# Sums of the later heads by ScalarE, six weight pieces in the attention instead of eight, gate mixtures ahead of weight steps

## The chip, the cores and the metric

The kernel runs on one core of one Trainium2 chip. The metric is the device time of one execution in microseconds; the median of three runs stands for a kernel.

## What is computed

The reference, cut to what matters:

```
# attention: batch 4, 8 heads, 576 tokens, head size 64, mask by blocks of 64 tokens
scores = where(block_i >= block_j, q @ k.T / 8, -1e9)
attn   = exp(scores - max(scores));  attn /= sum(attn) + 1e-9
x = attn @ v                                  # heads side by side: 2304 tokens x 512
# first feed-forward
xk = mu_k * x + (1 - mu_k) * x_prev           # x_prev: the token before
xr = mu_r * x + (1 - mu_r) * x_prev
x  = sigmoid(xr @ w_r) * (relu(xk @ w_k)**2 @ w_v)      # w_k 512x1024, w_v 1024x512
# second feed-forward
xn = (x - mean) / sqrt(var + 1e-6) * g_ln
out = x + relu(xn @ w_ch1) @ w_ch2            # w_ch1 512x2048, w_ch2 2048x512
```

## The kernel before

All products keep fp32 accuracy: an operand is split into a high part (rounded to fp32r) and the rest, and three products are added. The order of work is written by hand; every engine has its own queue and takes it in that order.

**Attention** (loop at L725). A unit is one head (`h`), with two joint units (`z`) for the first 64 tokens. Iteration i issues on TensorE the score product A of unit i+1 (`s<-kq`), product B of unit i (`s<-QK`), which adds the rests and the subtracted maximum, and the value product of unit i-1 (`p<-e,V`). VectorE makes the maxima of unit i+1: five reductions `part<-s`, one `r<-part`; ScalarE moves three quarters (`r<-r`), then VectorE makes `m<-r` and `QK<-m,s`, on which product B waits. ScalarE makes `e<-s`, the exponentials (`em_B`).

`norm` (L469) ends unit i-2. The value product's PSUM tile `p` holds 64 rows of values and 64 rows of sums. ScalarE copies the values to `U`; `sums` (L480) reduces the sums on VectorE to `rs<-p`. Heads come by twos (z = 0 and 1); with the second, ScalarE adds 1e-9 (`rs<-rs`), VectorE makes the reciprocal and spreads it (`RB`), and GpSimd multiplies (`XT<-U,RB`).

**Weight pieces** (`load_split`, L83). `w_r`, `w_k` and `w_v` are 20 pieces of 128x512, each split in five steps: `load` (a DMA of 0.5 MB on SyncE's queue into an int8 tile `raw`, of which there are two), `above` and `below` (two Relu forms of the exponent byte), `expo` (L124 or L126) and `bits` (L130), `high`, `low`. A `raw` tile is free again after `bits`. In the attention (`PIECES`, L659) a letter stands for a step and its place for the iteration: ScalarE has `above`, `below` and `high`, GpSimd `expo` and `low`, VectorE `bits`. Behind it VectorE has `above` (L112), `expo` (L124) and `bits`, ScalarE `below` (`p<-raw,ce`), GpSimd `high` (L134) and `low`. There `Convert.step` (L154) moves every piece on its way one step on and then starts the next one:

```
for j in self.going: ... f = j.pop(0) ...
if start and self.jobs: j = self.jobs.pop(0) ... j.pop(0)()
```

**Gate stage** (L819). Six groups of 384 tokens; `em_r(g)` is 36 matmuls (`s<-wr,x`), `out_r` the sigmoid. The mixtures of group g+1 (`prep`, L502) are made meanwhile, for four blocks kk: scale on ScalarE (`p<-XT`), add on VectorE (`mix`, L513), cast on ScalarE (`x<-mix`), subtraction (`x<-mix,x`) on VectorE for kk = 0, called `sub0` here, and on GpSimd for the others. Weight steps are `conv.step()`.

**Hidden stage** (L835). Per group four products `em_h` (24 matmuls, `s<-x,wk`, two PSUM tiles in turn), each with an output `out_h` (L532): ScalarE `a<-s`, `k<-a`, `a<-a`, VectorE `k<-a,k`, with one tile `a`; then three value products `em_v` (`p<-wv,k`). In the first group (j = 0) the last weight steps run between product and output (`conv.some(3)`). The second feed-forward follows.

Of the kernel before, what the change touches and what calls it, by code (L numbers as in the profile page):

```python
# [7 lines left out]
F32 = mybir.dt.float32  # L8
# [4 lines left out]
ALU = mybir.AluOpType  # L13
AX = mybir.AxisListType
# [7 lines left out]
NG = NTOK // GT  # L22
# [9 lines left out]
def attention_moe_kernel(ctx, tc, raw_d, dup_d, raw0_d, dup0_d, v_d, v0_d, msk_d, mz_d, vec_d, eye_d, wk_d, wv_d, wr_d, wc1_d, wc2_d, out_d):  # L32
    nc = tc.nc
    red = nc.vector.tensor_reduce
# [4 lines left out]
    def act(out, in_, func=AF.Copy, **kw):  # L39
        nc.scalar.activation(out=out, in_=in_, func=func, **kw)  # L40
# [4 lines left out]
    def opened(es, name, bufs=1, **kw):  # L45
        return es.enter_context(tc.tile_pool(name=name, bufs=bufs, reuse_waits="tile", **kw))
# [136 lines left out]
    cp = opened(es_a, "ac", 1, side=R)  # L183
# [4 lines left out]
    lq = opened(es_q, "ar", 3, side=R)  # L188
    V = [cp.tile([128, 1024], F32, name=f"V{i}") for i in range(2)]
    RB = cp.tile([128, 512], F32, name="RB")  # L190
    part = [cp.tile([128, 16, 5], F32, name=f"part{i}") for i in range(2)]
    NB = 3
    QK = [qp.tile([128, 1216], F32R, name=f"QK{i}") for i in range(NB)]
    QB, KL = [x[:, 0:576] for x in QK], [x[:, 576:1216] for x in QK]
    IZ = 14
# [181 lines left out]
    def v3(ap):  # L377
        return ap.rearrange("p (b i) -> p b i", i=32)
# [90 lines left out]
    def norm(u):  # L469

        n = u[1]
        b, h = divmod(n, H)
        z = h % 2
        p = T.pop(("p", u, 0))
        if z == 0:
            T["nm"] = [sp.tile([128, 16], F32, name=x) for x in ("rs", "r3")] + [sp.tile([128, 512], F32, name="U")]
        rs, r3, U = T["nm"]
        act(U[64 * z:64 * z + 64], p[64 - 64 * z:128 - 64 * z])

        def sums():  # L480
            half = slice(64 * z, 64 * z + 64)
            red(out=rs[half], in_=v3(p[half]), axis=AX.X, op=ALU.max, apply_transpose=True)
            if z:
                act(rs, rs, bias=1e-9)

        return [sums] if z == 0 else [
            sums,
            lambda: nc.vector.reciprocal(out=r3, in_=rs),
            lambda: nc.vector.transpose(out=RB, in_=r3.unsqueeze(2).to_broadcast([128, 16, 32])),
            lambda: nc.gpsimd.tensor_tensor(out=XT[b][:, h // 2, 65:577], in0=U, in1=RB, op=ALU.mult),  # L490
        ]
# [25 lines left out]
    def preps(g, c, X):  # L517
        return [lambda kk=kk: prep(g, kk, c, X) for kk in range(4)]
# [3 lines left out]
    def em_h(X, m0):  # L522
        s = ps.tile([128, 1536], F32, name="s")
        nm = 2
        for kk in range(4):
            for i in range(nm):
                m = m0 + i
                for x, (wi, xi) in enumerate(PASS):
                    mm(s[:, 512 * i:512 * i + GT], wk[wi][:, kk, 128 * m:128 * m + 128], X[xi][:, kk], kk == 0 and x == 0, kk == 3 and x == 2)
        return s  # L530

    def out_h(m0, s):  # L532
        nm = 2
        sv = s.rearrange("p (i n) -> p i n", n=512)[:, 0:nm, 0:GT]
        a = hp.tile([128, 2, GT], F32, name="a")
        act(a[:, 0:nm], sv, AF.Relu)
        act(k2[0][:, m0:m0 + nm], a[:, 0:nm], AF.Square)
        act(a[:, 0:nm], a[:, 0:nm], AF.Square)
        sub(nc.vector, k2[1][:, m0:m0 + nm], a[:, 0:nm], k2[0][:, m0:m0 + nm])

    def em_r(X):
        s = ps.tile([128, 1536], F32, name="s")
        for kk in range(4):
            for t in range(3):
                for x, (xi, wi) in enumerate(PASS):
                    mm(s[:, 512 * t:512 * t + 512], X[xi][:, kk, 128 * t:128 * t + 128], wr[wi][:, kk], kk == 0 and x == 0, kk == 3 and x == 2)
        return s

    def out_r(g, s):
        r = rp.tile([128, 3, DM], F32, name="r")  # L550
        act(r.rearrange("p t d -> p (t d)"), s, AF.Sigmoid)
        T["r", g] = r
        if g in HORD[3:]:
            nc.scalar.dma_start(out=r_scr[g], in_=r)

    def load_r(g, p):
        T["r", g] = r = p.tile([128, 3, DM], F32, name="r")
        nc.sync.dma_start(out=r, in_=r_scr[g])
# [5 lines left out]
    def em_v(g, t, store=True):  # L564
        p = pv.tile([128, 512], F32, name="p")
        for m in range(8):
            for x, (xi, wi) in enumerate(PASS):
                mm(p, k2[xi][:, m, 128 * t:128 * t + 128], wv[wi][:, m], m == 0 and x == 0, m == 7 and x == 2)
        r = T["r", g][:, t]
        st = rs6.tile([128, 6], F32, name="st")  # L570
        tt(out=r, in0=p, in1=r, op=ALU.mult)
        i = 3 * g + t
        if store:
            put_x(g, t)
        nc.vector.bn_stats(out=st, in_=r)
        nc.vector.bn_aggr(out=mv[:, i], in_=st)
# [6 lines left out]
    def chunk_jobs(c):  # L583
        L = []
        for k in (0, 2):
            w = wc1_d[128 * k:128 * k + 256, CF * c:CF * c + CF].rearrange("(a p) n -> p a n", a=2)
            L.append(load_split(w, lambda i, k=k: W[c % 2][0][i][:, k:k + 2]))
        for k in range(2):
            r0 = CF * c + 128 * k
            L += pieces(wc2_d[r0:r0 + 128], lambda i: W[c % 2][1][i], k, DM)  # L590
        return L
# [7 lines left out]
    def ln_scale(i0, i1):  # L599
        act(rsd[:, i0:i1], mv[:, i0:i1, 1], AF.Sqrt, bias=eps)  # L600
        nc.vector.reciprocal(out=rsd[:, i0:i1], in_=rsd[:, i0:i1])
# [37 lines left out]
    def em_c2(c, G, ts):  # L639
# [17 lines left out]


    PIECES = [  # L659
        (1, "l.12xbhw"), (4, "l12xbhw"), (7, "l.12xbhw"), (17, "l12xbhw"),  # L660
        (20, "l.12xbhw"), (23, "l12xbhw"), (26, "l.12xbhw"), (29, "l12xbhV"),
    ]


# [3 lines left out]
    with tc.manual_schedule():  # L668
# [9 lines left out]
        conv = Convert(jobs)  # L678
# [46 lines left out]
        for i in range(N + 2):  # L725
# [5 lines left out]
            if i + 4 < N:  # L731
                load_raw(units[i + 4])
                load_dup(units[i + 4])
            F = norm(units[i - 2]) if 0 <= i - 2 < N and units[i - 2][0] == "h" else []
            if i < N:
                em_B(units[i])
            if i == N - 2:
# [5 lines left out]
                xq = Convert(preps(0, MR, X2[0]) + preps(1, MR, X2[1]))  # L743
# [74 lines left out]
        T["free"] = True  # L818
        for g in range(NG):  # L819
            s = em_r(X2[g % 2])  # L820
            if g == 0:
                conv.step()
            else:
                Y = X2[(g - 1) % 2]
                xq = Convert(preps(g + 1, MR, Y) if g + 1 < NG else preps(HORD[0], MK, Y))
                xq.step()
                out_r(g - 1, s0)
                conv.step()
                xq.some(2)
                conv.step()  # L830
                xq.all()
            s0 = s
        T["free"] = False
        out_r(NG - 1, s0)
        for j, g in enumerate(HORD):  # L835
            for m0 in (0, 2, 4, 6):
                s = em_h(X2[j % 2], m0)
                if j == 0:
                    conv.some(3)
                out_h(m0, s)  # L840
                if j + 1 == NG and m0 == 0:
                    ln_scale(0, 3 * g)
                    ln_scale(3 * g + 3, NTILE)
            if j == 0:
                conv.all()
                T["beside"] = False
            if j + 1 == NG:
                break
            xq = Convert(preps(HORD[j + 1], MK, X2[(j + 1) % 2]))
            em_v(g, 0)  # L850
            xq.all()
            if j + 2 == NG:
                conv = Convert(chunk_jobs(0))
                conv.some(2, keep=2)
            em_v(g, 1)
            if j + 2 == NG:
                conv.some(2, start=False, keep=2)
            em_v(g, 2)
            if j < 2:
                load_r(HORD[j + 3], rp)  # L860
            elif j + 2 == NG:
                es_r.close()
                rp = opened(es_r, "rp2", 1, side=R)
                load_r(HORD[j + 1], rp)
# [7 lines left out]
        g = HORD[-1]  # L872
# [70 lines left out]
        for x, (c, G) in enumerate(steps):  # L943
# [10 lines left out]
            if G == GORD[0] and c + 1 < NC2:  # L954
                conv = Convert(chunk_jobs(c + 1))
# [68 lines left out]
```

## Time and profile before

| | us |
|---|---|
| median of 3 runs (859.73 to 860.23) | 860.21 |
| the profiled execution, its own time | 859.62 |
| its span | 857.8 |
| TensorE busy / VectorE / ScalarE / GpSimd | 823.1 / 519.8 / 387.0 / 265.4 |

The span is the time from the first to the last instruction of the profiled execution; 1.8 us of its own time lie around it. Busy times are sums over the whole span, so they say nothing about which stage waits: the attention runs to about 192 us, the gate to about 248, the first hidden group's value products begin at about 266. In the rows below a line is `start, length, engine, line, operation, out<-in, shapes, count`, and in brackets the idle time of the engine before it and what released it. PE is TensorE, DVE VectorE, ACT ScalarE, POOL GpSimd.

### The profile page before, as it was taken

To read this page: it belongs to the slowest core of one execution; us is meant where nothing else is said; L and a number is where in the kernel's file an instruction comes from. 1 tells how busy PE (TensorE), PEld (TensorE's weight loads), DVE (VectorE), ACT (ScalarE), POOL (GpSimd) and SP (SyncE) were. 2 spreads that over 40 slices of the span, in tenths; PEclk is the share of its full clock that TensorE was granted. 3 is DMA by queue.
4 is the path that set the end of the run, shared out by engine and by line. 5 is a ranking of instruction groups with operands and counts; after the bars stand their busy time and mean duration, and the time that the engine had idled before them with its cause. 6 is when DMAs were issued, how large, how long until landed. Compare 5 with 4: busy or idle time off the path is not lost. (4 is left out here: it accounts for less than half of the span.)

```text
span 857.8 us, 10477 instructions
## 1 busy us (share of the span) xinstructions
PE 823.1 (96%) x3828; PEld 670.5 (78%) x3828; DVE 519.8 (61%) x920; ACT 387.0 (45%) x674; POOL 265.4 (31%) x229
## 2 busy tenths in 40 slices
PE   4988999999989999999999999999999999999998
PEld 3655666558768989989988878888888888888886
DVE  6899799998785243252567665556364555546443
ACT  5876687778756335335553433232131222223110
POOL 6788678855773010110120320101010010101000
PEclk9999999999999999999999999999999999999999
DMA  9995666722530110010525031111020111101023
GB/s 241 314 309 187 198 205 218 233 66 75 182 99 13 61 55 32 25 37 12 210 74 184 1 98 50 49 42 58 1 72 27 50 50 50 50 4 46 1 99 123
DMA packets 40068, 83.65 MB, mean 98 GB/s; under 512 B 3472, under 2 KB 17936, under 8 KB 40016
## 3 DMA queue, kind: packets, MB, share of 16 engines
q1 hardware_dynamic: 34544, 60.61, 21.6%
q0 software_dynamic: 5040, 20.01, 7.8%
q10 hardware_dynamic: 432, 2.36, 0.7%
q8 instruction: 30, 0.49, 0.2%
q14 instruction: 22, 0.18, 0.1%
HBM read 71.17 MB, written 11.80 MB: 97 GB/s over the span
## 5 line engine op out<-in xcount | busy, mean ns | idle before, releaser
L344 PE MATMUL ph<-xn,c 128*128 128x512 f32 (+1 forms) x960 | 205.6, 369 | 0.0
L344 PE MATMUL po<-c,h 128*128 128x512 f32 x864 | 204.1, 391 | 0.4 <-DVE acc L651 0.4
L344 PEld LDWEIGHTS ph<-xn,c 128*128 128x128 f32 x960 | 167.9, 188 | 31.8
L344 PEld LDWEIGHTS po<-c,h 128*128 128x128 f32 x864 | 161.6, 188 | 35.3 <-DVE acc L651 0.8
L40 ACT ACTIVATE h<-ph 128x512 fp32r<-128x512 f32 (+1 forms) x80 | 42.8, 551 | 220.3 <-PE ph L344 220.3
L43 POOL TENSOR_TENSOR c<-a,c 128x512 fp32r<-128x512 f32 x32 | 42.0, 1313 | 310.2 <-ACT c L40 239.8
L637 DVE SCALAR_TENSOR_TENSOR h<-ph,h 128x512 fp32r<-128x512 f32 (+1 forms) x80 | 49.8, 636 | 129.2 <-ACT h L40 129.2
L651 DVE TENSOR_TENSOR acc<-po,acc 128x512 f32<-128x512 f32 x144 | 97.8, 688 | 45.9 <-PE po L344 43.7
L344 PE MATMUL s<-x,wk 128*128 128x384 f32 x576 | 103.1, 338 | 2.2 <-DVE x L43 1.8
L344 PEld LDWEIGHTS s<-x,wk 128*128 128x128 f32 x576 | 101.4, 188 | 3.6 <-DVE x L43 2.1
L344 PE MATMUL p<-e,V 128*128 128x512 f32 (+4 forms) x320 | 103.7, 453 | 0.0
L344 PE MATMUL p<-wv,k 128*128 128x512 f32 x432 | 99.7, 390 | 0.6 <-DVE k L43 0.6
L344 PEld LDWEIGHTS p<-wv,k 128*128 128x128 f32 x432 | 80.8, 188 | 17.5 <-DVE k L43 1.0
L344 PEld LDWEIGHTS p<-e,V 128*128 128x128 f32 (+1 forms) x320 | 53.3, 190 | 43.9 <-issue 36.7
L43 POOL TENSOR_TENSOR x<-mix,x 128x384 fp32r<-128x384 f32 x36 | 40.4, 1135 | 152.6 <-ACT x L40 149.2
L40 ACT ACTIVATE a<-raw,ce 128x512 f32<-128x512 int8 (+1 forms) x80 | 57.0, 750 | 60.6 <-DVE a L130 58.5
L43 DVE TENSOR_TENSOR k<-a,k 128x768 fp32r<-128x768 f32 x24 | 23.4, 976 | 81.7 <-ACT a L40 81.7
L399 DVE TRANSPOSE_TENSOR_REDUCE part<-s 128x14 f32<-128x448 f32 (+4 forms) x160 | 65.1, 465 | 1.1
L130 DVE SCALAR_TENSOR_TENSOR a<-raw,a 128x512 int32<-128x512 int32 x52 | 53.8, 1035 | 3.9 <-POOL wv L43 0.4
L40 ACT ACTIVATE e<-s 128x1536 f32<-128x1536 f32 (+1 forms) x34 | 48.4, 1425 | 14.8 <-PE s L344 7.9
L344 PE MATMUL s<-wr,x 128*128 128x512 f32 x216 | 51.0, 396 | 2.7 <-DVE x L43 2.7
L344 PEld LDWEIGHTS s<-wr,x 128*128 128x128 f32 x216 | 40.5, 188 | 12.8 <-DVE x L43 3.6
(110 smaller groups left out, 839.4 us busy)
## 6 DMA issues: line engine op xcount, KB each, us to landing
kq<-in_dup_dram POOLq DMA_DIRECT2D x15, 1088.0 KB, 5.9
raw<-in_raw_dram SPq DMA_DIRECT2D x32, 288.0 KB, 4.7
raw<-in_w_ch_dram SPq DMA_DIRECT2D x16, 511.6 KB, 3.6
raw<-in_w_ch_dram SPq DMA_DIRECT2D x32, 255.6 KB, 3.1
V<-in_v_dram SPq DMA_DIRECT2D x16, 320.0 KB, 5.6
x_scr<-r SPq DMA_DIRECT2D x18, 256.0 KB, 2.0
acc<-x_scr SPq DMA_DIRECT2D x18, 256.0 KB, 4.7
out_dram<-acc SPq DMA_DIRECT2D x18, 256.0 KB, 2.0
```

The source lines that it names most:

```text
L40: nc.scalar.activation(out=out, in_=in_, func=func, **kw)
L43: eng.tensor_tensor(out=out, in0=in0, in1=in1.bitcast(F32), op=ALU.subtract)
L130: stt(out=st["a2"].bitcast(I32), in0=w3, scalar=5, in1=st["a1"].bitcast(I32), op0=ALU.logical_shift_right, op1=ALU.bitwise_or)
L344: nc.tensor.matmul(out=out, lhsT=lhsT, rhs=rhs, start=start, stop=stop, **kw)
L399: red(out=pt[0:kp, b0:b0 + w // 32, j], in_=v3(s[0:kp, o:o + w]), axis=AX.X, op=ALU.max, apply_transpose=True)
L637: stt(out=h1[1][:, m, 0:n], in0=p[:, 0:n], scalar=0.0, in1=h1[0][:, m, 0:n].bitcast(F32), op0=ALU.max, op1=ALU.subtract)
L651: tt(out=acc[i], in0=p, in1=acc[i], op=ALU.add)
```

## The change

For heads n >= 14 (`far`) ScalarE copies the rows of sums as well, with the 1e-9 added, to its half of a new SBUF tile `SM`; the first head of a pair has no sum step, and the second reduces all 128 rows of `SM` at once. In the attention six pieces are split instead of eight. At the gate the first three mixtures stand ahead of the first weight step and the second step comes behind the last mixture; in the first hidden group two weight steps instead of three stand ahead of each output.

```diff
--- before.py
+++ after.py
@@ -188,6 +188,7 @@
     lq = opened(es_q, "ar", 3, side=R)
     V = [cp.tile([128, 1024], F32, name=f"V{i}") for i in range(2)]
     RB = cp.tile([128, 512], F32, name="RB")
+    SM = cp.tile([128, 512], F32, name="SM")
     part = [cp.tile([128, 16, 5], F32, name=f"part{i}") for i in range(2)]
     NB = 3
     QK = [qp.tile([128, 1216], F32R, name=f"QK{i}") for i in range(NB)]
@@ -477,13 +478,21 @@
         rs, r3, U = T["nm"]
         act(U[64 * z:64 * z + 64], p[64 - 64 * z:128 - 64 * z])
 
+
+        far = n >= IZ
+        if far:
+            act(SM[64 * z:64 * z + 64], p[64 * z:64 * z + 64], bias=1e-9)
+
         def sums():
+            if far:
+                red(out=rs, in_=v3(SM), axis=AX.X, op=ALU.max, apply_transpose=True)
+                return
             half = slice(64 * z, 64 * z + 64)
             red(out=rs[half], in_=v3(p[half]), axis=AX.X, op=ALU.max, apply_transpose=True)
             if z:
                 act(rs, rs, bias=1e-9)
 
-        return [sums] if z == 0 else [
+        return [sums][far:] if z == 0 else [
             sums,
             lambda: nc.vector.reciprocal(out=r3, in_=rs),
             lambda: nc.vector.transpose(out=RB, in_=r3.unsqueeze(2).to_broadcast([128, 16, 32])),
@@ -657,8 +666,8 @@
 
 
     PIECES = [
-        (1, "l.12xbhw"), (4, "l12xbhw"), (7, "l.12xbhw"), (17, "l12xbhw"),
-        (20, "l.12xbhw"), (23, "l12xbhw"), (26, "l.12xbhw"), (29, "l12xbhV"),
+        (1, "l.12xbhw"), (4, "l12xbhw"), (7, "l.12xbhw"),
+        (17, "l12xbhw"), (22, "l.12xbhw"), (26, "l.12xbhw"),
     ]
 
 
@@ -818,17 +827,17 @@
         T["free"] = True
         for g in range(NG):
             s = em_r(X2[g % 2])
-            if g == 0:
-                conv.step()
-            else:
+            if g:
                 Y = X2[(g - 1) % 2]
                 xq = Convert(preps(g + 1, MR, Y) if g + 1 < NG else preps(HORD[0], MK, Y))
                 xq.step()
                 out_r(g - 1, s0)
+                xq.some(3)
+            conv.step()
+            if g:
+                xq.all()
+            if 0 < g < NG - 1:
                 conv.step()
-                xq.some(2)
-                conv.step()
-                xq.all()
             s0 = s
         T["free"] = False
         out_r(NG - 1, s0)
@@ -836,7 +845,7 @@
             for m0 in (0, 2, 4, 6):
                 s = em_h(X2[j % 2], m0)
                 if j == 0:
-                    conv.some(3)
+                    conv.some(2)
                 out_h(m0, s)
                 if j + 1 == NG and m0 == 0:
                     ln_scale(0, 3 * g)
```

How the queues change, at three places.

VectorE in the gate stage, group g = 4, before. `mix` are the mixtures' adds, `x11` the subtraction `sub0`, `a1` and `a2` the exponent and the piece's bits, `raw8` a piece's bytes:

```order
L513 SCALAR_TENSOR_TENSOR mix_2216<-XT3_93,omm_61,p_2217 128x384
L513 SCALAR_TENSOR_TENSOR mix_2233<-XT3_93,omm_61,p_2234 128x384
L124 SCALAR_TENSOR_TENSOR a1_2225<-a1_2225,p_2228 128x512
L130 SCALAR_TENSOR_TENSOR a2_2227<-raw8_2162,a1_2225 128x512
L112 TENSOR_SCALAR a1_2245<-raw8_2230 128x512
L43 TENSOR_TENSOR x11_1747<-mix_2216,x10_1746 128x384
L513 SCALAR_TENSOR_TENSOR mix_2238<-XT3_93,omm_61,p_2239 128x384
L513 SCALAR_TENSOR_TENSOR mix_2255<-XT3_93,omm_61,p_2256 128x384
L124 SCALAR_TENSOR_TENSOR a1_2245<-a1_2245,p_2248 128x512
L130 SCALAR_TENSOR_TENSOR a2_2247<-raw8_2230,a1_2245 128x512
L112 TENSOR_SCALAR a1_2310<-raw8_2250 128x512
```

and of the change:

```order
L522 SCALAR_TENSOR_TENSOR mix_2197<-XT3_93,omm_61,p_2198 128x384
L522 SCALAR_TENSOR_TENSOR mix_2203<-XT3_93,omm_61,p_2204 128x384
L43 TENSOR_TENSOR x11_1733<-mix_2197,x10_1732 128x384
L522 SCALAR_TENSOR_TENSOR mix_2208<-XT3_93,omm_61,p_2209 128x384
L124 SCALAR_TENSOR_TENSOR a1_2153<-a1_2153,p_2156 128x512
L130 SCALAR_TENSOR_TENSOR a2_2155<-raw8_2140,a1_2153 128x512
L112 TENSOR_SCALAR a1_2221<-raw8_2158 128x512
L522 SCALAR_TENSOR_TENSOR mix_2214<-XT3_93,omm_61,p_2215 128x384
L124 SCALAR_TENSOR_TENSOR a1_2221<-a1_2221,p_2224 128x512
L130 SCALAR_TENSOR_TENSOR a2_2223<-raw8_2158,a1_2221 128x512
L112 TENSOR_SCALAR a1_2238<-raw8_2226 128x512
```

`sub0` and the third add went ahead of the first weight step (`expo`, `bits`, `above`), and between the two weight steps only the fourth add is left.

ScalarE in the first hidden group, before. `r` is the last sigmoid, `p<-raw8` a `below`, `a<-s` the step of an output that frees the PSUM tile:

```order
L40 ACTIVATE r_2349<-s_2264 128x1536
L40 ACTIVATE p_2383<-raw8_2335,ce_64 128x512
L40 ACTIVATE p_2394<-raw8_2385,ce_64 128x512
L40 ACTIVATE a_2400<-s_2351 128x768
L40 ACTIVATE k20_1876<-a_2400 128x768
L40 ACTIVATE a_2400<-a_2400 128x768
L40 ACTIVATE a_2433<-s_2405 128x768
L40 ACTIVATE k20_1876<-a_2433 128x768
L40 ACTIVATE a_2433<-a_2433 128x768
```

and of the change:

```order
L40 ACTIVATE r_2319<-s_2245 128x1536
L40 ACTIVATE p_2353<-raw8_2311,ce_64 128x512
L40 ACTIVATE p_2364<-raw8_2355,ce_64 128x512
L40 ACTIVATE a_2368<-s_2321 128x768
L40 ACTIVATE k20_1857<-a_2368 128x768
L40 ACTIVATE a_2368<-a_2368 128x768
L40 ACTIVATE p_2405<-raw8_2366,ce_64 128x512
L40 ACTIVATE p_2416<-raw8_2407,ce_64 128x512
L40 ACTIVATE a_2420<-s_2373 128x768
L40 ACTIVATE k20_1857<-a_2420 128x768
L40 ACTIVATE a_2420<-a_2420 128x768
L40 ACTIVATE p_2457<-raw8_2418,ce_64 128x512
```

Two further `below` copies now stand between the first output and the second, and one ahead of the third; they belong to the two pieces that left the attention and to one that the gate no longer reaches.

ScalarE in the attention, one iteration from unit 19's `e` back to the step before it, before. `a1` is an `above`, `QK` the copy for a later unit:

```order
L40 ACTIVATE a1_1096<-raw8_1039,ce_64 128x512
L40 ACTIVATE QK2_131<-kq_959 64x512
L40 ACTIVATE U_1072<-p_1101 64x512
L40 ACTIVATE e_1119<-s_134 128x1536
L40 ACTIVATE r4_1126<-r4_1126 32x16 x3
L40 ACTIVATE rs_1070<-rs_1070 128x16
```

and of the change:

```order
L40 ACTIVATE a1_1097<-raw8_1040,ce_64 128x512
L40 ACTIVATE QK2_132<-kq_960 64x512
L40 ACTIVATE U_1073<-p_1102 64x512
L40 ACTIVATE SM_127<-p_1102 64x512
L40 ACTIVATE e_1121<-s_135 128x1536
L40 ACTIVATE r4_1128<-r4_1128 32x16 x3
L40 ACTIVATE a2_1141<-raw8_1040,ce_64 128x512
```

The copy to `SM` stands between `U` and `e`; the addition to `rs` is gone.

## Rows read from the trace of the kernel before

**Rows 1.** Waits of TensorE, whole span: us in total, times, longest us.
```profile
PE s L344 <- DVE QK L432: 12.3, 14, 2.1
...
PE s L344 <- DVE x L43: 4.5, 3, 2.0
```

**Rows 2.** Timeline of all engines, iterations 25 and 26 of the attention.
```profile
149.01 1.46 DVE L130 SCALAR_TENSOR_TENSOR a<-raw,a 128x512 int32<-128x512 int32 x1
...
153.47 0.70 DVE L482 TRANSPOSE_TENSOR_REDUCE rs<-p 64x16 f32<-64x512 f32 x1
...
153.65 0.71 ACT L40 ACTIVATE r<-r 32x16 f32<-32x16 f32 x3 [1.89 <-DVE r L404]
...
154.40 0.21 DVE L430 TENSOR_REDUCE m<-r 32x16 f32<-32x64 f32 x1 [0.23 <-ACT r L40]
...
155.38 0.50 PE L344 MATMUL s<-QK 128*128 128x512 f32 x1 [1.33 <-DVE QK L432]
```

**Rows 3.** Timeline of ScalarE, then of TensorE, iterations 28 and 29.
```profile
166.26 0.59 ACT L40 ACTIVATE U<-p 64x512 f32<-64x512 f32 x1
...
166.88 1.45 ACT L40 ACTIVATE e<-s 128x1536 f32<-128x1536 f32 x1
...
168.36 0.71 ACT L40 ACTIVATE r<-r 32x16 f32<-32x16 f32 x3
...
165.44 1.05 PE L344 MATMUL s<-QK 128*128 128x512 f32 x5 [0.53 <-DVE QK L432]
...
170.15 0.62 PE L344 MATMUL s<-QK 128*128 128x512 f32 x2
```

**Rows 4.** Timeline at the gate: `sub0` twice, a group of matmuls.
```profile
226.69 0.55 DVE L43 TENSOR_TENSOR x<-mix,x 128x384 fp32r<-128x384 f32 x1
...
227.30 8.63 PE L344 MATMUL s<-wr,x 128*128 128x512 f32 x36 [0.74 <-DVE x L43]
...
236.50 1.33 DVE L43 TENSOR_TENSOR x<-mix,x 128x384 fp32r<-128x384 f32 x1
```

**Rows 5.** Groups by line and form, gate: count, busy us, mean ns, idle before.
```profile
L130 DVE SCALAR_TENSOR_TENSOR a<-raw,a 128x512 int32<-128x512 int32 x13 | 11.2, 863 | 1.1 <-POOL wv L43 0.4
...
L112 DVE TENSOR_SCALAR a<-raw 128x512 f32<-128x512 int8 x12 | 10.5, 878 | 1.2 <-DMA raw<-in_w_v_dram 0.8
...
L513 DVE SCALAR_TENSOR_TENSOR mix<-XT,omm,p 128x384 f32<-128x384 f32 x16 | 9.8, 609 | 6.4 <-ACT p L40 5.0 <-POOL wk L43 0.7 <-POOL wv L43 0.7
...
L124 DVE SCALAR_TENSOR_TENSOR a<-a,p 128x512 int32<-128x512 f32 x12 | 8.2, 681 | 0.2
...
L40 ACT ACTIVATE p<-XT,vec 128x384 f32<-128x384 f32 x16 | 9.3, 581 | 8.1 <-DVE mix L513 8.0
...
L40 ACT ACTIVATE p<-raw,ce 128x512 f32<-128x512 int8 x12 | 8.7, 723 | 4.9 <-DMA raw<-in_w_v_dram 3.1 <-ACT r L40 0.9 <-DVE a L112 0.5
...
L40 ACT ACTIVATE r<-s 128x1536 f32<-128x1536 f32 x6 | 8.6, 1439 | 0.0
```

**Rows 6.** Instructions on the tile raw, 200 to 262 us: its DMAs.
```profile
DMA to landing us min/median/max: 3.4/3.5/4.3
```

**Rows 7.** Page, costliest groups: hidden products.
```profile
L344 PE MATMUL s<-x,wk 128*128 128x384 f32 x576 | 103.1, 338 | 2.2 <-DVE x L43 1.8
```

**Rows 8.** Timeline of the first hidden group.
```profile
255.40 0.74 ACT L40 ACTIVATE p<-raw,ce 128x512 f32<-128x512 int8 x1 [3.09 <-DMA raw<-in_w_v_dram]
...
256.08 0.79 ACT L40 ACTIVATE a<-s 128x768 f32<-128x768 f32 x1
...
258.67 1.10 DVE L43 TENSOR_TENSOR k<-a,k 128x768 fp32r<-128x768 f32 x1 [0.19 <-ACT a L40]
...
271.08 4.15 PE L344 MATMUL p<-wv,k 128*128 128x512 f32 x17 [0.59 <-DVE k L43]
```

**Rows 9.** Stretches: length, busy of PE, PEld, DVE, ACT, POOL, PEclk, DMA, GB/s.
```profile
84.20:86.30 2.10, 0.02 (x1) 0.05 (x1) 1.81 (x5) 1.76 (x5) 2.02 (x3) 1.00 0.55 156
...
86.30:89.70 3.40, 3.40 (x8) 2.13 (x9) 1.83 (x2) 1.70 (x3) 3.25 (x4) 0.50 0.79 229
```

## The prediction

> **What bounds the kernel now.** I read the waits of TensorE first, over the whole span: it waits for VectorE in two places, for `QK` in the attention (14 waits, 12.3 us) and for `x`, the first mixture of a group, at the gate's end (3 waits, 4.5 us) [rows 1]. After the first hidden group nothing of note is waited for, so the change can only act in these two stages and on whatever it makes late behind them. Then I read the timeline around such waits, to see which engine's queue the late instruction stood in.
>
> In an attention iteration whose chain TensorE waits for, VectorE's queue is `part` reductions, `r`, sums, `m`, `QK`. The reader is to see in [rows 2] what `m` waited for: the sums ran from 153.47 to 154.17, but ScalarE's three `r` copies ended at 154.36 and `m` began at 154.40. **The sums lie in the shadow of ScalarE's copies.** The long wait there, 1.33 us, comes from the iteration before, where the weight step's `bits` (L130) took 1.46 us ahead of `RB`; a like wait with no `bits` before it is 0.53 [rows 3].
>
> At the gate, `sub0` (VectorE's first `x` subtraction) comes in VectorE's queue behind a whole weight step. It takes 0.55 us at one time and 1.33 at another [rows 4], and a group of matmuls (8.63 us) starts right after it.
>
> **The change, part by part.**
>
> *Sums by ScalarE (18 heads).* Added on ScalarE: 18 copies of 64x512, each as long as `U`, 0.59 [rows 3], 10.6 us in all; removed: 9 small `rs` copies and, on VectorE, 9 of 18 sums (0.70 each, 6.3 us). The removed sums lay in the shadow just shown, so TensorE gains 0 from them. The kept sum reads 128 partitions in SBUF instead of 64 in PSUM, in the same shadow: 0; even at twice the 0.70 it would stick out of the shadow by 0.5 in each of eight pairs of heads, the price of rival 3. The copy stands ahead of `e`. Where ScalarE is idle before `e` it costs nothing. Where it is not (an iteration with both `high` and `above`), `U` ran 166.26 to 166.85, `e` followed at 166.88, the `r` copies right at its end at 168.36, and TensorE took the next `QK` matmul at 170.15 [rows 3]; all of that moves by 0.59, of which about 0.1 was slack. Of the eight odd iterations from 19 to 33 only the one after such an iteration has this; in the others either the removed pieces free ScalarE or TensorE has 0.4 us of slack at that point. So +0.5, with bounds 0 and 8 x 0.5 = 4.
>
> *Two pieces fewer in the attention.* A piece that moves takes along its load on SyncE's queue, `bits` on VectorE, three copies on ScalarE, `expo` and `low` on GpSimd; at the gate and behind it the same piece is `above`, `expo`, `bits` on VectorE, `below` on ScalarE, `high`, `low` on GpSimd and again a load. The piece whose `bits` made the 1.33 wait is gone: 1.33 - 0.53 = -0.8. The other stood at the end of the attention, where the value products of the last heads and the first gate group keep TensorE running: 0, and if that cover were gone, its `bits`, at most 1.46. **Attention in all: -0.3** (bounds -0.8 and +3.2).
>
> *Gate stage.* Per group the order is now: scale 0, sigmoid, mixtures 0 to 2, first weight step, mixture 3, second weight step. Both steps are there (none is removed before g = 5), but now stand almost back to back, and they share two `raw` buffers: the load that the second step's `above` and `below` read is issued when the first step's `bits` free a buffer. Between them VectorE has `above` 0.88, a mixture's add 0.61, `expo` 0.68 and `bits` 0.86 [rows 5], 3.0 us; a load takes 3.4 to 4.3, median 3.5 [rows 6]. So ScalarE and VectorE wait there, ahead of the next group's scale. From one sigmoid to the next: sigmoid 1.44, scale 0.58, add 0.61, `sub0` 0.55, add 0.61, `expo` 0.68, `bits` 0.86, load 3.5, `below` 0.72, scale 0.58 [rows 4 to 6], and seven hand-overs of 0.05 (as from 154.36 to 154.40 in [rows 2]): **10.5 us a group, against TensorE's 8.63.** Without gate waits the group that starts at 227.30 would start at 226.56 (its wait is 0.74), so gate group 1 ends at 209.3 and group 5 at 243.8 [rows 4]. The sigmoids then start at 209.4, 219.9, 230.4 and 240.9. `sub0` of the first hidden mixtures ends 1.44 + 0.58 + 0.61 + 0.55 + 0.2 later, at 244.3: TensorE waits 0.5. The last mixture comes after add 0.61, `expo` 0.68, `bits` 0.86, `above` 0.88, add 0.61, cast 0.5 to 0.6 and a subtraction of up to 1.33, at 250.0, and the last quarter of the first hidden product (24 matmuls in 4.3 us, [rows 7]) follows: end at 251.1 instead of 248.1. The 4.5 us of waits are replaced by 3.0.
>
> *Hidden stage, first group.* Here the eight remaining weight steps now go two before each of the four outputs, where before all `below` copies stood ahead of the first output and ended with one late load (3.09 us idle on ScalarE [rows 8]). The `below` copies stand in ScalarE's queue ahead of the output that frees a PSUM tile, and each second one needs a load that waits for `bits` behind the output before. The chain: adds done 247.9; `expo`, `bits` to 249.5; load to 253.0; `below` to 253.8; output 0, from 256.08 to 259.77 before [rows 8], 3.69 us, to 257.5; `expo`, `bits` to 259.0; load to 262.5; `below` to 263.3; first step of output 1, 0.79, to 264.1. The fourth product needs the tile which that step frees, while the third ends at 251.1 + 2 x 4.3 = 259.7: **a wait of 4.4 us.** Then output 1 to 267.0, `expo`, `bits`, `above`, `expo`, `bits` 4.0 to 271.0, subtraction 1.1 [rows 8] to 272.1, output 3 to 275.8. Before, TensorE had this last piece at 271.08 [rows 8]. **From the end of the attention to here: +4.7.** By waits: -4.5 + 3.0 + 4.4 and some 2 more in the first value product.
>
> *Landing.* Five loads lie on this chain (three groups, two in the hidden stage). At 3.4 us each the stretch is +4.2, at 4.3 it is +8.7. I take 3.7, nearer the median than the longest: +1.0, **+5.7**.
>
> **The sum.** -0.3 + 5.7 = +5.4. Against the profiled execution's own 859.62 that is 865.0; the median of the three runs, 860.21, lies 0.6 above that execution, so I forecast **865.6**. A measurement of this kernel can tell about 0.2%, 1.7 us, from no change. This case reaches from 862 (the short `bits` and `above` of a quiet GpSimd in the hidden stage, some 2 us, and loads of 3.4) to 869 (loads of 4.3).
>
> **A rule against the trace.** `sub0` took 0.55 and 1.33 [rows 4], and I use 0.55, since in the new order it stands ahead of the weight step. The Trainium skill ("SBUF — State Buffer", section "Who interferes with whom") says that a VectorE operation with two SBUF inputs and a GpSimd operation that reads SBUF shut each other out for their whole length. The previous group's `low` pieces on GpSimd could then meet `sub0` anyway: by the rule 0.8 more in each of three groups, 868.0 (rival 5); by the row taken, 865.6.
>
> **Rivals.**
>
> 1. *Faster: the loads are hidden.* If a load lands within the 3.0 us between the steps, a group costs VectorE 4 x 0.61 + 0.55 + 2 x 2.42 = 7.8 us, under 8.63, and the gate's 4.5 us go. Then output 0 can start at 248.1, its load is there at 256.3, the fourth product waits 1.1, and output 3 ends at 269.5: -1.6 against 271.08, with the attention -1.9, 858.3; if the outputs too are not held up, -4.8, 855.4. The point that decides is a landing of 3.0 us. For it: all three gate waits are for `x` behind a weight step [rows 1]. Against it: no load landed under 3.4 [rows 6].
> 2. *No change: the gate's gain and the hidden stage's loss even out*, about 860. That needs ScalarE and VectorE to come out of the gate about 3 us earlier than worked out here, as if `bits` and `above` always ran at their shortest.
> 3. *Slower still: `e` late for every head*, +4 in the attention instead of +0.5: 869. Against it: in [rows 2] ScalarE stood idle 1.89 us before `r`.
> 4. *Slower still: the clock.* After TensorE's idle stretch of 84.2 to 86.3 its granted clock was at 0.50, the lower of its two levels (1.2 GHz), for the next 3.4 us [rows 9]; that costs 1.7 us. The wait of 4.4 us before the fourth product is longer. I count it as 0, because the value product that follows has to wait for the outputs anyway; if it isn't absorbed, 867.3. The Trainium skill ("TensorE: Matmul & The Clock Gate", section "HAM oscillation — how this bites in real kernels") has the same: a product that waits long for its data starts again at the lower clock. By that the row would repeat here.
> 5. *Slower still: `sub0` meets GpSimd* in every group, 1.33 instead of 0.55 [rows 4]: 3 x 0.8 more, 868.0. The 1.33 shows that it happens; but before, `sub0` stood later in the group than now, beside the next subtractions.
>
> **How the numbers follow.** Forecast case 0.53, `sub0` late 0.06, clock not absorbed 0.09, `e` late for all 0.09, no change 0.11, faster 0.12. Slower by over 0.2% is 0.53 + 0.06 + 0.09 + 0.09 = 0.77. The range 859 to 871 leaves out the faster rival and a small rest above; the forecast case's own range is 862 to 869.
>
> **What would show it.** Right: in the attention, `m` still starts at the end of the `r` copies and one wait for `QK` of about 1.3 is gone; at the gate no wait for `x` within the groups, but sigmoids 10 to 11 us apart and waits in the first hidden product; a wait of 4 to 6 us before the fourth hidden product, released by ScalarE, whose `below` before output 1 is released by a DMA. Wrong: no such wait, or `below` before output 1 idle for under 1 us. If several waits for `QK` have grown by 0.5, the copies of `SM` were the cause and rival 3 holds.

## The result, and the profile after

The changed kernel takes **867.16 us** (median of four runs, 866.36 to 867.91) against 860.22 for the kernel before, measured on the same chip: a ratio of 1.0077 (95% interval 1.0063 to 1.0091), or 5.4 to 7.8 us slower. The forecast was 865.6, with 859 to 871 as its range. The profiled execution is the one of 867.91; its span is 866.1 against 857.8.

TensorE's waits, whole span (line waited for, us in total, times, longest), beside [rows 1]:

```profile
PE s L345 <- DVE QK L433: 11.6, 14, 2.1
PE s L345 <- ACT wk L40: 10.1, 1, 10.1
PE s L345 <- ACT a L40: 5.6, 2, 5.0
PE s L345 <- ACT x L40: 2.0, 2, 1.2
...
PE s L345 <- DVE x L43: 0.3, 1, 0.3
```

The 4.5 us for `x` by VectorE have shrunk to 0.3, 2.0 for ScalarE's `x` have come, and a line that was not there before stands third: 5.6 us for `a`, the step of a hidden output that frees a PSUM tile. The 10.1 for `wk` is the very first wait of the program. It was 9.0 in the profile of before and lay between 9.0 and 9.7 in the experiments' profiles, so up to 1.1 us of the difference between the two spans is not the change's.

TensorE's timeline from the last gate group to the first value product (start, length; idle before it and releaser in brackets):

```profile
236.00 8.92 PE L345 MATMUL s<-wr,x 128*128 128x512 f32 x36 [0.81 <-ACT x L40]
246.07 0.44 PE L345 MATMUL s<-x,wk 128*128 128x384 f32 x1 [1.16 <-ACT x L40]
246.81 1.31 PE L345 MATMUL s<-x,wk 128*128 128x384 f32 x6 [0.30 <-DVE x L43]
248.50 9.01 PE L345 MATMUL s<-x,wk 128*128 128x384 f32 x41 [0.38 <-POOL x L43]
258.09 4.49 PE L345 MATMUL s<-x,wk 128*128 128x384 f32 x24 [0.58 <-ACT a L40]
267.57 6.58 PE L345 MATMUL s<-x,wk 128*128 128x384 f32 x24 [4.99 <-ACT a L40]
...
279.10 12.09 PE L345 MATMUL p<-wv,k 128*128 128x512 f32 x52 [0.42 <-DVE k L43]
```

The fourth hidden product waits 4.99 us, and the piece of the value product that started at 271.08 before [rows 8] starts at 279.10. The same stretch on ScalarE:

```profile
210.48 1.44 ACT L40 ACTIVATE r<-s 128x1536 f32<-128x1536 f32 x1
...
220.43 0.74 ACT L40 ACTIVATE p<-raw,ce 128x512 f32<-128x512 int8 x1 [2.48 <-DMA raw<-in_w_k_dram]
...
221.91 1.44 ACT L40 ACTIVATE r<-s 128x1536 f32<-128x1536 f32 x1
...
233.61 1.43 ACT L40 ACTIVATE r<-s 128x1536 f32<-128x1536 f32 x1
...
243.68 1.44 ACT L40 ACTIVATE r<-s 128x1536 f32<-128x1536 f32 x1
...
266.07 0.72 ACT L40 ACTIVATE p<-raw,ce 128x512 f32<-128x512 int8 x1 [5.44 <-DMA raw<-in_w_v_dram]
266.73 0.79 ACT L40 ACTIVATE a<-s 128x768 f32<-128x768 f32 x1
```

The sigmoids (`r<-s`) of the middle groups come 11.4, 11.7 and 10.1 us apart. In each of these groups one `below` (`p<-raw`) waits 2 to 2.5 us for its load. In the hidden group one waits 3.26 ahead of output 0 and one 5.44 ahead of output 1, right before the `a<-s` that TensorE waits for. The 8.3 us between the two spans are 1.1 at the start of the program, -0.4 in the attention, 7.3 from the first gate matmul to the last piece of the value product (279.10 here, 271.08 before) and 0.3 behind it.

### The profile page after: what moved, and what is told of

It reads as the page before. It is cut to its first block, busy times and chain, and to the rows that moved or that the text cites. A ratio compares the mean times of both kernels' runs of the same rounds, so it can differ in the third digit from the quotient of the medians.

```text
span 866.1 us, 10494 instructions
## 1 busy us (share of the span) xinstructions
PE 827.8 (96%) x3828; PEld 673.7 (78%) x3828; DVE 513.8 (59%) x914; ACT 393.9 (45%) x679; POOL 263.9 (30%) x230
## 5 line engine op out<-in xcount | busy, mean ns | idle before, releaser
L345 PE MATMUL s<-x,wk 128*128 128x384 f32 x576 | 107.1, 347 | 7.4 <-ACT a L40 5.6
L345 PEld LDWEIGHTS s<-x,wk 128*128 128x128 f32 x576 | 104.6, 194 | 9.7 <-ACT a L40 6.2
L40 ACT ACTIVATE a<-raw,ce 128x512 f32<-128x512 int8 (+1 forms) x76 | 54.1, 751 | 61.0 <-DVE a L130 58.5
L40 ACT ACTIVATE a<-s 128x768 f32<-128x768 f32 x24 | 19.5, 811 | 66.4 <-PE s L345 63.4
```

Source lines behind the costliest of these rows:

```text
L345: nc.tensor.matmul(out=out, lhsT=lhsT, rhs=rhs, start=start, stop=stop, **kw)
```

## Experiments

Each kernel was timed beside the kernel before on the same chip; that one's median was 859.36 to 859.46 in these sets, and differences are taken to it. The first four hold the parts of the change, one by one and two together.

**The sums alone.** The kernel before with `SM`, the copies and the sums by twos; nothing else.

```diff
+    SM = cp.tile([128, 512], F32, name="SM")
+        if far:
+            act(SM[64 * z:64 * z + 64], p[64 * z:64 * z + 64], bias=1e-9)
...
-        return [sums] if z == 0 else [
+        return [sums][far:] if z == 0 else [
```

> The kernel before with the sums by ScalarE alone (eight pieces, old gate order). Theory A (the change costs time by loads that the second of two weight steps waits for): the attention moves by +0.5 us at most, 860.2 to 861.0. Rival, the copies to SM delay every far head's exponentials: +4 us, 864. A third reading, VectorE's queue is shorter by nine sums and the chain of QK gains from it: 858 to 859.

Measured: 861.76, ratio 1.0028 (1.0017 to 1.0038), +2.3. Neither theory had that size. In its profile 1.5 us of it lie in the attention (worked out in the next section) and 0.7 between the first gate matmul and the second hidden group (91.4 us instead of 90.7). The last experiment returns to it.

**The pieces alone.** The kernel before with the six `PIECES` of the change; two more pieces are left for later, in the old order.

```diff
-        (1, "l.12xbhw"), (4, "l12xbhw"), (7, "l.12xbhw"), (17, "l12xbhw"),
-        (20, "l.12xbhw"), (23, "l12xbhw"), (26, "l.12xbhw"), (29, "l12xbhV"),
+        (1, "l.12xbhw"), (4, "l12xbhw"), (7, "l.12xbhw"),
+        (17, "l12xbhw"), (22, "l.12xbhw"), (26, "l.12xbhw"),
```

> The kernel before with six pieces in the attention instead of eight, sums and gate order as before. Theory A: the attention gains 0.8 us, but two pieces more are left for the first hidden group, and three below copies with two raw buffers stand ahead of output 0; one more expo, bits, load, below round (5.7 us) delays it, TensorE waits about 5 us before the third product, and the time is about 864 to 865. Rival, the arithmetic of two pieces hides behind the products wherever it is put: 859.4.

Measured: 863.39, ratio 1.0039 (1.0027 to 1.0052), +3.9. Its ScalarE, first hidden group:

```profile
252.80 0.72 ACT L40 ACTIVATE p<-raw,ce 128x512 f32<-128x512 int8 x1 [2.61 <-DMA raw<-in_w_v_dram]
256.17 0.72 ACT L40 ACTIVATE p<-raw,ce 128x512 f32<-128x512 int8 x1 [2.64 <-DMA raw<-in_w_v_dram]
256.83 0.79 ACT L40 ACTIVATE a<-s 128x768 f32<-128x768 f32 x1
```

Two late loads stand ahead of output 0 and TensorE waits for it, as expected, but 2.3 us and not 5; a further 1.8 us of waits for `k` came in the first value product.

**The gate order alone.** The kernel before with the new gate loop and two steps ahead of each hidden output.

```diff
-            if g == 0:
-                conv.step()
-            else:
+            if g:
...
+                xq.some(3)
+            conv.step()
+            if g:
+                xq.all()
+            if 0 < g < NG - 1:
                 conv.step()
-                xq.some(2)
-                conv.step()
-                xq.all()
...
-                    conv.some(3)
+                    conv.some(2)
```

> The kernel before with the new gate order and two steps ahead of each hidden output, eight pieces and the old sums. Theory A: the gate's waits of 4.5 us become about 2.7 us as in the change's own trace, and with two pieces fewer behind the attention only one below copy stands between outputs 0 and 1, whose load comes in time, so the wait of 5 us before the fourth product goes: 858 to 860. Rival, the new order itself makes the wait before the fourth product: 865 to 866.

Measured: 861.74, ratio 1.0026 (1.0017 to 1.0035), +2.3. The wait before the fourth product is gone, as theory A says, and yet the kernel is slower: the gate still waits (1.35 and 1.14 us), and now the first value product waits 0.68 + 1.08 us for the last outputs. That second bound was not in the forecast.

**Sums and pieces, old gate order.** The two edits above together.

```diff
+        if far:
+            act(SM[64 * z:64 * z + 64], p[64 * z:64 * z + 64], bias=1e-9)
...
+        (17, "l12xbhw"), (22, "l.12xbhw"), (26, "l.12xbhw"),
```

> Sums by ScalarE and six pieces, with the old gate order and three steps ahead of each hidden output. If the parts add up: 859.5 + 2.3 + 3.9 = 865.7, and the reordering of the change costs about 1 to 2 us more. If the reordering is the main cost with six pieces (its wait of 5 us before the fourth product has no like here): 861 to 863.

Measured: 863.66, ratio 1.0051 (1.0039 to 1.0064), +4.3. The time lies between the two expectations. By the medians the sums add 0.4 with six pieces (4.3 - 3.9), not the 2.3 that they cost with eight, and the new gate order adds the remaining 2.6. Each interval is about 2 us wide, so these medians alone do not separate 0.4 from 0 or from 1; the profiles do it in the next section.

**A third raw buffer.** The change with every third piece behind the attention loaded into a further tile: at the gate one in the memory that `k2` takes later, in the hidden group the three mixture buffers, idle there. All instructions stand in the same order.

```diff
-            st["raw"] = raw = stg2.tile([128, 4096], I8, name="raw8")
+            T["nraw"] = T.get("nraw", 0) + 1
+            more = T.get("more") if T["nraw"] % 3 == 0 else None
+            st["raw"] = raw = more() if more else stg2.tile([128, 4096], I8, name="raw8")
...
+        third = opened(es_g, "third", 1, side=R)
+        T["more"] = lambda: third.tile([128, 4096], I8, name="raw8")
...
+        T["more"] = lambda: MIX.bitcast(I8)[:, 0:4096]
```

> The change with every third weight piece behind the attention in a further raw buffer (three instead of two), all instructions in the same order. Theory A (loads that are issued only when bits free a buffer): the late loads land in time, the gate's waits go and the wait before the fourth product goes with them: 855.5 to 858.5. Rival, the work of VectorE and ScalarE in the two stages is too much, loads or not: 864 to 867.

Measured: 858.26, ratio 0.9986 (0.9975 to 0.9996). From 1.0077 to 0.9986 is 7.8 us, by one buffer. Its eleven executions lie between 856.70 and 860.43, at mean granted clocks from 0.998 to 0.994; the profile is of one at 0.994 (859.65). Its TensorE:

```profile
242.53 17.06 PE L347 MATMUL s<-x,wk 128*128 128x384 f32 x96
260.29 3.49 PE L347 MATMUL p<-wv,k 128*128 128x512 f32 x14 [0.70 <-DVE a L126]
265.13 1.20 PE L347 MATMUL p<-wv,k 128*128 128x512 f32 x4 [1.35 <-DVE k L43]
267.00 1.19 PE L347 MATMUL p<-wv,k 128*128 128x512 f32 x2 [0.67 <-POOL wv L43]
268.78 14.40 PE L347 MATMUL p<-wv,k 128*128 128x512 f32 x52 [0.59 <-DVE k L43]
```

All four hidden products run without a wait, and the value product begins 5.5 us ahead of the kernel before (260.29 against 265.75). Then it waits 3.3 us in four pieces and its last 52 matmuls take 14.40 instead of the change's 12.09, so that the next group starts at 283.02, where it did before (283.00). VectorE explains the waits:

```profile
261.90 0.69 DVE L126 SCALAR_TENSOR_TENSOR a<-a,p 128x512 int32<-128x512 f32 x1
262.69 1.52 DVE L132 SCALAR_TENSOR_TENSOR a<-raw,a 128x512 int32<-128x512 int32 x1
264.13 0.94 DVE L43 TENSOR_TENSOR k<-a,k 128x768 fp32r<-128x768 f32 x1
267.76 0.96 DVE L43 TENSOR_TENSOR k<-a,k 128x768 fp32r<-128x768 f32 x1 [2.69 <-ACT a L40]
```

The subtraction of output 2 stands behind a weight step, and output 3 cannot begin before it, because both use the one tile `a`. ScalarE shows that wait:

```profile
265.17 0.81 ACT L40 ACTIVATE a<-s 128x768 f32<-128x768 f32 x1 [2.87 <-DVE k L43]
```

**The same without the sums.** Six pieces, new order, third buffer.

```diff
-        if far:
-            act(SM[64 * z:64 * z + 64], p[64 * z:64 * z + 64], bias=1e-9)
```

> Six pieces, the gate order of the change and the third raw buffer, with the old sums: after_all3 without the copies to SM. If these copies cost 2 us in themselves, as their run alone showed, 856; if that was their effect on the gate's waits, which the third buffer takes away, 0.3 to 1 us less than after_all3: 857.3 to 858.

Measured: 857.55, ratio 0.9977 (0.9967 to 0.9986): by the medians 0.7 less than with the sums, the second expectation. The two intervals overlap, but the profiles agree with it: the attention is 0.8 shorter than with the sums, and from the first gate matmul to the second hidden group both take 91.0 us.

**The same with eight pieces.** New order, third buffer, old sums.

```diff
+        (20, "l.12xbhw"), (23, "l12xbhw"), (26, "l.12xbhw"), (29, "l12xbhV"),
```

> The gate order of the change with eight pieces in the attention, the old sums, and a third raw buffer behind the attention. Theory A, refined (late loads first; where these are gone, VectorE's own weight steps ahead of the last hidden output): two pieces fewer lie on VectorE behind the attention, so neither the gate nor the first value product waits: 854.5 to 856. Rival, VectorE's work is the bound in any case: 858 to 860.

Measured: 857.63, ratio 0.9984 (0.9976 to 0.9993): between the two. The gate no longer waits; the first hidden product has 1.3 us of short waits for `x`, and the value product still waits (0.7 for ScalarE's `k`, 1.1 for VectorE's), with two pieces fewer on VectorE. Its last two subtractions:

```profile
264.94 0.96 DVE L43 TENSOR_TENSOR k<-a,k 128x768 fp32r<-128x768 f32 x1 [2.70 <-ACT a L40]
268.59 0.96 DVE L43 TENSOR_TENSOR k<-a,k 128x768 fp32r<-128x768 f32 x1 [2.69 <-ACT a L40]
```

VectorE is idle for 2.7 us ahead of each, so its own work isn't what delays these two; the subtraction before them, at 261.30, did stand behind a weight step. These outputs come 3.65 us apart, ScalarE's steps and VectorE's subtraction by turns: the single `a` was left as suspect.

**The third buffer in the kernel before.**

```diff
+            st["raw"] = raw = more() if more else stg2.tile([128, 4096], I8, name="raw8")
```

> The kernel before with the third raw buffer alone. If the gate's waits of 4.5 us come from sub0 standing behind a weight step (order), they stay and only ScalarE's idle time in the hidden group goes: 858.5 to 859.5. If they come from late loads, the buffer alone takes them away: 855.

Measured: 863.94, ratio 1.0052 (1.0039 to 1.0065). This run answers another question than it asked. With eight pieces the count made the first load behind the attention take the new tile; its memory was the attention's until 203.7, and the load, issued at 189.17 before, was issued then:

```profile
208.37 0.73 ACT L40 ACTIVATE p<-raw,ce 128x512 f32<-128x512 int8 x1 [4.53 <-DMA raw<-in_w_k_dram]
```

**The same, first for the third load,** and at the gate alone.

```diff
-            more = T.get("more") if T["nraw"] % 3 == 0 else None
+            more = T.get("more") if T["nraw"] % 3 == 2 else None
```

> The kernel before with a third raw buffer in the gate stage alone, taken for the third load behind the attention and every third after it (before_all3 took it for the first, which then waited for the attention's tiles to come free). If the gate's waits of 4.5 us come from sub0 standing behind a weight step (order), they stay: 859 to 860. If they come from late loads, the buffer takes them away: 855 to 856.

Measured: 859.32, ratio 0.9999 (0.9990 to 1.0007), with the same three waits for `x` as in [rows 1] (0.73, 1.96, 1.76). So in the old order the gate's waits are a matter of order: `sub0` behind a weight step. In the new order they are a matter of loads. Either cure alone gains nothing (the order alone: +2.3).

**Order, buffer and a second tile `a`.** Eight pieces, old sums, new order, third buffer at the gate; in the first hidden group two of the four outputs use the mixture buffers as their `a`.

```diff
-        a = hp.tile([128, 2, GT], F32, name="a")
+        if T.get("beside") and m0 % 4:
+            a = MIX[:, 0:2 * GT].rearrange("p (i n) -> p i n", n=GT)
+        else:
+            a = hp.tile([128, 2, GT], F32, name="a")
```

> Eight pieces, old sums, the gate order of the change, a third raw buffer at the gate (for the third load on), and in the first hidden group a second tile a, so that an output need not wait for VectorE's subtraction of the one before. If the waits in the first value product (1.75 us in gate8_all3) come from that one tile: 855 to 856.5. If they come from VectorE's weight steps alone: 857.5 as gate8_all3.

Measured: **852.43**, ratio 0.9921 (0.9908 to 0.9934), the fastest of all, 6.9 us under the kernel before and better than expected. It differs from the version of 857.63 in two more things: its first load behind the attention isn't held up by the new tile, and the hidden group has two raw buffers again. Gone are the 1.75 us for the last outputs, and 1.3 us of short waits for GpSimd's mixtures in the first hidden product; which of the three edits took the latter was not tried apart. In the two profiles the second hidden group starts at 275.29 instead of 281.52, 6.2 earlier: 0.9 of it ahead of the first gate matmul, where this execution kept the full clock and the other did not (last section), 0.5 in the gate, 2.3 in the hidden products and 2.6 in the value products. The gain over the kernel before isn't one of clock: at a mean granted clock of 0.998 this kernel took 853.04 and 853.29 and that one 858.88 to 859.67, at 1.00 851.96 and 858.66. Its TensorE has no gap from the gate into the value product:

```profile
224.61 17.43 PE L346 MATMUL s<-wr,x 128*128 128x512 f32 x74
241.88 17.22 PE L346 MATMUL s<-x,wk 128*128 128x384 f32 x96
258.94 9.26 PE L346 MATMUL p<-wv,k 128*128 128x512 f32 x40
```

**Seven pieces in that kernel.** The piece whose `bits` made the 1.33 us wait [rows 2] is left out in the attention.

```diff
-        (20, "l.12xbhw"), (23, "l12xbhw"), (26, "l.12xbhw"), (29, "l12xbhV"),
+        (23, "l12xbhw"), (26, "l.12xbhw"), (29, "l12xbhV"),
```

> gate8_a2 with seven pieces in the attention: the one whose bits stand in iteration 25 is left out there and converted behind it. The attention gains 0.8 to 1.2 us. If VectorE has room for one more piece behind it (2.4 us): 854.5 to 855.5. If not, the value product waits for it and gives the gain back: 856 to 858.

Measured: 858.54 (854.11 to 860.54), ratio 0.9982 (0.9968 to 0.9997), above both expectations. The attention did gain 1.1. One more piece behind it, with two raw buffers in the hidden group, and the change's wait before the fourth product is back, at 2.5 us:

```profile
255.24 0.71 ACT L40 ACTIVATE p<-raw,ce 128x512 f32<-128x512 int8 x1 [3.72 <-DMA raw<-in_w_v_dram]
255.90 0.79 ACT L40 ACTIVATE mix<-s 128x768 f32<-128x768 f32 x1
```

That profile is of the execution of 854.11. Two executions had a mean granted clock of 1.00 (854.11 and 854.59), 2.2 to 2.6 above the version with eight pieces at that clock (851.96); in the other ten the clock was 0.996 or lower, down to 0.991 for 860.54. What those lost where was not seen in a profile, so of the 6.1 us between the medians only the 2.2 to 2.6 are put down to the piece.

**The sums in the fastest kernel.**

```diff
+        if far:
+            act(SM[64 * z:64 * z + 64], p[64 * z:64 * z + 64], bias=1e-9)
```

> gate8_a2 with the sums by ScalarE added. By the trace of sums_alone their price is in the attention, where two iterations that have both high and above ahead of the exponentials became 0.7 us longer each: 852.4 + 0.3 to 1.0 = 852.7 to 853.4. By its median (2.3 us over before) the copies cost more, wherever they stand: 854.5 to 855.

Measured: 854.85, ratio 0.9950 (0.9935 to 0.9964), 2.4 more than without: the second expectation. ScalarE, two exponentials in a row, first with the sums and then in the kernel without:

```profile
160.24 1.45 ACT L40 ACTIVATE e<-s 128x1536 f32<-128x1536 f32 x1 [0.27 <-ACT SM L40]
...
166.83 1.45 ACT L40 ACTIVATE e<-s 128x1536 f32<-128x1536 f32 x1
```

```profile
160.21 1.45 ACT L40 ACTIVATE e<-s 128x1536 f32<-128x1536 f32 x1 [0.99 <-DVE RB L491]
...
165.91 1.45 ACT L40 ACTIVATE e<-s 128x1536 f32<-128x1536 f32 x1
```

This iteration lasts 6.59 instead of 5.70. In all the gate stage starts 1.3 us later (192.69 against 191.35). The rest came in the first hidden product, whose mixtures by GpSimd were late twice (0.9 us of waits, none without the sums); why there was not tried.

## Why the prediction was right, step by step

**The attention, -0.3: right.** TensorE's first gate matmul is at 193.06 instead of 192.32, 0.74 later, of which 1.1 come from the start of the program: -0.4 for the attention. Two places of the changed kernel's timeline, all engines around a sum by twos, then ScalarE in iterations 28 and 29:

```profile
147.64 0.70 DVE L488 TRANSPOSE_TENSOR_REDUCE rs<-SM 128x16 f32<-128x512 f32 x1
...
148.34 0.72 ACT L40 ACTIVATE r<-r 32x16 f32<-32x16 f32 x3
...
149.09 0.21 DVE L431 TENSOR_REDUCE m<-r 32x16 f32<-32x64 f32 x1 [0.75 <-ACT r L40]
...
155.40 1.04 PE L345 MATMUL s<-QK 128*128 128x512 f32 x5 [0.46 <-DVE QK L433]
```

```profile
161.19 1.45 ACT L40 ACTIVATE e<-s 128x1536 f32<-128x1536 f32 x1 [0.37 <-ACT SM L40]
...
167.62 1.45 ACT L40 ACTIVATE e<-s 128x1536 f32<-128x1536 f32 x1
```

The sum ended at 148.34, and `m` came at the end of ScalarE's `r` at 149.09: the sums do lie in the shadow, as in [rows 2]. The wait of 1.33 [rows 2] is 0.46 now: -0.9, where -0.8 was worked out. In the iteration with `high` and `above` the next `e` came 6.43 us after the one before instead of 5.72: +0.7, where +0.5 was. The last iteration ahead of the gate, which the prediction did not count, grew too, from 5.56 (181.16 to 186.72) to 6.13 (181.95 to 188.08), but the first gate matmul then came 4.98 behind its exponentials instead of 5.60.

The two parts can be told apart across all profiles, because kernels with the same attention agree within 0.1 us from one exponential (at 105.17 before, at 106.31 in the change) to the first gate matmul. This stretch takes 87.1 to 87.2 us with eight pieces and the old sums (six profiles), 86.0 to 86.1 with six pieces and the old sums (two), 86.7 to 86.8 with six pieces and the copies (three), 88.6 with eight pieces and the copies (two). So the pieces gave -1.1, and the copies took 0.7 with six pieces and 1.5 with eight: the reason given for taking one iteration alone, that in others the removed pieces free ScalarE, is borne out. Both terms were somewhat too small, -0.8 and +0.5, and as they have opposite signs their sum hid it. Rival 3 (+4 in the attention) falls.

**The gate: right in its mechanism, mis-sized in one term.** The waits came to 0.81 + 1.16 + 0.30 + 0.38 = 2.7 against 3.0 forecast. There are none in the groups before the last; that one waited 0.81, where no wait was forecast. The term "10.5 us a group" (10.7 with the landing of 3.7 that was taken) measured 11.4, 11.7 and 10.1:

```profile
223.38 0.33 ACTq L563 DMA_DIRECT2D r_scr<-r  x1
223.75 0.88 ACT L40 ACTIVATE p<-XT,vec 128x192 f32<-128x192 f32 x2 [0.40 <-ACT r L40]
...
236.25 0.59 ACT L40 ACTIVATE p<-XT,vec 128x384 f32<-128x384 f32 x1 [0.30 <-DVE mix L522]
```

Three things made the two longer ones. Behind the sigmoid ScalarE issues a store of its result (`r_scr<-r`), and ahead of the next scale it is idle for 0.40; the third interval has no such store, and the prediction's chain had none. The load that the second step waits for landed after 4.0, 3.7 and 3.5 us. And where the 384 tokens lie in two batches, scales and adds run in two parts of 192, 0.88 instead of the 0.58 used for each scale and 0.74 instead of 0.61 for an add: in the second interval for all but its last scale, in the first for its last scale alone. [rows 5] show whole blocks alone. Over the three intervals that is 33.2 us instead of 32.1, +1.1.

**The hidden group: right.** Forecast: a wait of 4.4 us before the fourth product, released by ScalarE, whose `below` ahead of output 1 is released by a DMA. Measured: 4.99, `a`, and 5.44 for the load. What freed that load's buffer is VectorE's `bits` behind output 0:

```profile
261.66 0.69 DVE L130 SCALAR_TENSOR_TENSOR a<-raw,a 128x512 int32<-128x512 int32 x1
```

They ended at 262.35, SyncE issued the load at 262.43, it landed 3.6 us later, and `below` started at 266.07. From the first gate matmul to the last piece of the value product it was 86.0 us instead of 78.8: +7.3 where +5.7 was forecast. Of the 1.6 between, 1.1 are the gate intervals above, 0.3 lie ahead of them (17.4 us from the first gate matmul to the first of these sigmoids, where 17.1 was worked out) and 0.1 behind them. The landing taken, 3.7, was the median of the loads in this stretch; the five on the chain took 4.0, 3.7, 3.5, 4.2 and 3.6.

**The clock (rival 4): it fell, and was absorbed, as counted.** Stretches (length, busy of PE, PEld, DVE, ACT, POOL, granted clock, DMA share, GB/s):

```profile
248.50:257.50 9.00, 9.00 (x41) 8.39 (x41) 7.28 (x9) 4.45 (x7) 7.64 (x7) 0.82 0.46 126
...
262.56:267.55 4.99, 0.02 (x1) 0.00 (x0) 3.91 (x4) 1.45 (x2) 3.91 (x4) 0.78 0.57 176
267.55:271.00 3.45, 3.43 (x11) 3.43 (x12) 1.60 (x4) 2.96 (x4) 0.00 (x0) 0.50 0.12 49
```

After the idle stretch the granted clock was at 0.50, the 1.2 GHz level, and the fourth product took 6.58 us where the third had taken 4.49. Yet the value product waited 0.42 for `k` in the end, and the output behind that `k` had itself not waited for the fourth product but for VectorE:

```profile
275.49 0.81 ACT L40 ACTIVATE a<-s 128x768 f32<-128x768 f32 x1 [2.56 <-DVE k L43]
```

So a faster product would only have waited longer. The clock also fell once before, behind the gate's waits: 41 matmuls of the first two products took 9.01 us, at a mean clock of 0.82. That was absorbed too, by the third product's wait of 0.58 for `a`, which would have been longer. In the version with three buffers nothing absorbed it: its 52 matmuls of 14.40 us ran at a mean clock of 0.69 for the 6 us from 270 on. The Trainium skill ("TensorE: Matmul & The Clock Gate", section "HAM oscillation — how this bites in real kernels") says that a product that waits long for its data starts at the lower clock; here, after 4.99 us, it did.

**Rival 1 (faster, the loads hidden) names the right condition.** No load landed in the 3.0 us between the steps. With a third buffer, which lets them start earlier, the kernel was faster by 1.2 us (859.45 to 858.26); its nearer end, worked out for hidden loads, was 1.9. **Rival 2** (gain and loss even out) fell with the wait of 4.99. **Rival 5 fell:** `sub0` took 0.55 in every group of the new order; GpSimd was idle then, so the rule weighed there was not put to the test.

## What to carry to other kernels

Moving a step ahead of another moves its transfer too: ask of each step which buffer its load goes into and which instruction frees that buffer, and work out the distance between that instruction and the first reader. A wait can have two causes in series (here an order, and behind it two buffers); curing one alone gains nothing, which is no proof that it wasn't a cause. Look along the chain for the next single tile before trying: here `a`. Its second copy, together with a first load that no longer came late and two raw buffers in the hidden group, turned a gain of 1.7 us into one of 6.9; how much of that is the copy alone was not measured.

## What had not been expected

The same idle stretch in the attention, at the same point of the program, was followed by the clock at 0.50 in the profile of before [rows 9], and at full clock in that of the fastest kernel:

```profile
84.02:86.06 2.04, 0.04 (x1) 0.00 (x0) 1.75 (x5) 1.70 (x5) 1.97 (x3) 1.00 0.54 161
86.06:89.50 3.44, 3.40 (x13) 2.04 (x14) 1.93 (x3) 2.39 (x5) 3.29 (x4) 1.00 0.72 220
```

After an idle stretch of about 2 us, then, one execution loses clock and another does not. Of the fourteen profiles nine lost 1.7 us of full clock there and five nothing. Nor was 1.7 the price: the exponentials near 105 us started 95.6 to 96.6 us behind the first matmul in the nine and 95.0 to 95.2 in the five, 0.9 apart on average, because part of the loss went into waits. Two single profiles can differ by that much without any change. And the reduction of 128 partitions in SBUF took 0.70, as long as that of 64 in PSUM [rows 2].
